# Gated linear attention with an ELU feed-forward on one core: late form for spans 4 and 5, another weight decode, another way to k over P, another order

## The chip, the cores and the metric

One core of one Trainium2 chip runs the whole program. The metric is device time in microseconds, the median of the runs shown. The kernel before takes 504.29 us (503.95 to 504.69, three runs).

## The reference

Attention with a decaying state, then a feed-forward block. For each of 4 x 8 heads, over 768 positions with head size 48:

```python
for t in range(S):
    state = alpha[:, :, t, :, None] * state + np.einsum('bhd,bhe->bhde', k[:, :, t], v[:, :, t])
    y[:, :, t] = np.einsum('bhd,bhde->bhe', q[:, :, t], state)
...
h = x @ w_in                                   # x: 3072 x 384, w_in: 384 x 2048
g = np.where(h > 0.0, h, np.exp(np.minimum(h, 0.0)) - 1.0)
return g @ w_out                               # w_out: 2048 x 384
```

`x` is the attention's output, the heads side by side. The arrays are float32, but the drawn weights are float64, and the kernel gets the float64 words.

## The kernel before, in words

**Attention by spans.** The 768 positions of a batch element are six spans of 128, so there are 24 spans, numbered 0 to 23. A span works on all eight heads at once, in four slices of two heads. Within it P is the running product of alpha (SC, L200, on DVE); k is divided by P and put in a form with the kernel's sign conventions (LN, EX on ACT; KA, KB on DVE or POOL; KC on DVE, L232), q is multiplied by P (SQ, L249 or L252). S multiplies k and q (PE, L330 or L314), MK masks the result (DVE, L347 or L342), U multiplies k, laid over rows, with v (PE, L376 or L358), UA, UB and UC move the state on (L393, L395, L424, L426), and Y gives the span's output (PE, L437 or L442), which XH and XL split in a high and a low float32r part (L496, L522) and XD (L529, a DMA) completes.

**Two forms.** `EARLY`, `QU` and `QS` are 6: spans 0 to 5 take the early form, in which a Y product is split in two, one for the state and one for the mask part (L437), and U and S run over one PSUM bank each. From span 6 on the late form runs Y as one product over 128 rows (L442), and U and S as four products at a time on the four quarters of the array (`U4`, `S4`, L358 and L314), but the masks, the state's steps and SQ come in halves of 48 or 64 rows, so that DVE issues them twice, and MK four times (L342).

**k over rows.** U wants k with positions on the rows. In spans 0 to 5 that is TP (PE, L266) and a copy (KN, ACT, L295). From span 6 on it is `blocks` (L276): DVE transposes 32-row blocks, 16 instructions a span, called as TA, TB or T.

**Feed-forward by blocks.** Two spans are one block of 256 positions, so there are 12 blocks b; the 2048 hidden units are eight parts j. A(b, j) is 18 products (L639), O(b, j) 12 (L690); between them RA and RB (ACT, L647, L652), RC (DVE, L657), GH (ACT, L663) and GL (DVE, L676) make the ELU and its high and low parts. Z writes a block's result.

**Weights.** F (L549) loads 768 KB of float64 words for each of 16 weight parts, two to a pair p of eight. DA, DB and DC (DVE, L565, L571, L577) put a float32 together from the two 32-bit halves of each word, for a whole pair at a time; WH (ACT, L603) and WL (POOL, some on DVE or ACT, L623, L621) split it in high and low parts. LC, CA and CB (L585, L590, L595) load all weights once more in 32 pieces and check their range on ACT; V and VP gather the checks.

**Order.** Nothing is scheduled on the chip or by a planner at build time. `START` and `STEADY` are tables of step names with arguments; the steps are called in that order, and each engine and each queue executes its instructions in the order in which they were called. `STEADY` describes one block's worth of work, with numbers relative to the block, and is repeated. All input DMAs are on SP's queue. X is a product of a constant into a spare bank that nobody reads (L126); it occupies PE before the first data have come. PSUM has eight buffers and the spans' q, k and alpha share three, so a step can also wait for a buffer.

Of the kernel before, what the change touches and what calls it, by code (L numbers as in the profile page):

```python
# [30 lines left out]
EARLY = 6  # L31
# [3 lines left out]
QU, QS = 6, 6  # L35

PAIRS = 10

# [14 lines left out]
WH.4 SC.4 WL.4 Y3.2 Y.2 UA.3 PC.3 RB.0.0 MK.3 XH.2 DA.3 SQ.4 DC.1 DB.3 YL.3 LN.4 XL.2 Y3.3 UB.3 A.0.2 LV.4
WH.3 EX.4 F.10 CA.0 F.8 WL.3 Y.3 A.0.3 XH.3 UC.3 DC.3 XL.3 L.5 F.12 RA.0.1 KA.4 KB.4 A.1.1 A.1.0 LV.5 F.11
RC.0.0 RB.0.1 RC.0.1 WH.7 GH.0.0 SC.5 DA.5 RA.0.2 GH.0.1 A.1.2 RB.0.2 DB.5 RA.1.0 KC.4 RC.0.2 WH.1 RB.1.0 F.14
GH.0.2 GL.0.0 RC.1.0 WL.1 RA.1.1 GL.0.2 A.1.3 RA.0.3 GL.0.1 RB.0.3 TP.4 UB.0 DA.4 PC.4 RB.1.1 WL.7 WH.5 KN.4
O.0.0 RC.0.3 O.0.1 GH.0.3 DB.4 U.4 WL.5 GL.0.3 RC.1.1 DC.4 RA.1.3 GH.1.1 S.4 LN.5 O.0.2 O.0.3 RB.1.3 DC.5 LV.6
L.6 WH.8 MK.4 UB.4 RA.1.2 EX.5 LV.7 GH.1.0 UA.4 RB.1.2 WL.8 GL.1.0 WH.9 KA.5 RC.1.2 CB.0 A.0.4 GH.1.2 GL.1.1
UC.4 WH.10 KB.5 RA.0.4 KC.5 O.1.0 RC.1.3 TP.5 GL.1.2 SQ.5 GH.1.3 LC.1 DA.6 CA.1 KN.5 WH.11 L.7 O.1.1 DB.6
RB.0.4 WL.10 U.5 PC.5 RC.0.4 GL.1.3 GH.0.4 UA.5 A.1.4 A.0.5 SC.6 RA.1.4 WL.11 LN.6 EX.6 KA.6 WL.9 DC.6 F.15  # L60
RB.1.4 RA.0.5 O.1.2 GL.0.4 WH.14 O.1.3 RC.1.4 RB.0.5 RC.0.5 GH.0.5 GH.1.4 S.5 KB.6 SC.7 KC.6 WH.12 Y.4 O.0.4
WL.12 GL.1.4 PC.6 LN.7 EX.7 WL.14 MK.5 GL.0.5 F.13 A.0.6 TB.6 A.0.7 CB.1 L.8 RA.0.6 A.1.5 DA.7 KA.7 TA.6 DB.7
# [18 lines left out]
MK.2.1 UC.2 XD.1 ZV.4 O.-4 XD.0 RC.-3 CB.-12 SC.4 RB.-2 A.-1 PC.3 GH.-3 RC.-2 A.0 LN.4 GL.-3 UA.3 EX.4 RA.-1
GH.-2 LC.-11 MK.3.0 L.6 MK.3.1 UB.3 CA.-11 A.1 RA.0 KA.4 L.5 RB.-1 GL.-2 RC.-1 A.2 RB.0 UC.3 CB.-11 RA.1 GH.-1
RC.0 O.-3 KB.4 RB.1 SC.5 KC.4 LC.-10 GL.-1 LN.5 GH.0 EX.5 RC.1 T.4.1 O.-2 A.3 VP.0 CA.-10 T.4.2 GL.0 GH.1 A.4
T.4.3 KA.5 O.0 RA.2 GL.1 RB.2 RA.3 CB.-10 LV.5 RC.2 PC.4 GH.2 KB.5 RB.3 GL.2 LC.-9 O.1 O.-1 KC.5 RA.4 O.2 SQ.4
T.5.2 CA.-9 RB.4 RC.3 CB.-9 RC.4 GH.3 T.5.1 GH.4 T.5.0 GL.3 T.4.0 T.5.3 LC.-8 SQ.5 Z.-1 GL.4
"""

@with_exitstack
def gla_elu_ffn(ctx: ExitStack, tc: tile.TileContext, qka, vv, vn, wgt, out):
    nc = tc.nc  # L90
# [861 lines left out]
```

## Time and profile before

| what | value |
|---|---|
| median of three runs | 504.29 us |
| the profiled execution itself | 503.54 us |
| its span, first to last instruction | 501.8 us |
| granted TensorE clock, mean | 1.000 |
| PE, DVE, ACT, POOL busy, share of the span | 98%, 77%, 58%, 26% |
| the chain of waits, share of PE | 95% |
| lines L639 and L690 in that chain | 40% and 40% |
| DMA, mean over the span | 122 GB/s |

The span is the time between the first and the last instruction; the execution's own time, 503.54, is 1.7 us longer. A busy PE is one that has a matmul in flight. The chain of waits goes back from the last instruction, at each step to what released it.

### The profile page before, as it was taken

What the parts mean: (1) busy time and instruction counts of PE and PEld (TensorE: products, weight loads), DVE (VectorE), ACT (ScalarE), POOL (GpSimd) and SP (SyncE); (2) the same over time, 40 slices, a digit from 0 to 9 for tenths busy, and PEclk for the clock granted to TensorE, in tenths of its full rate; (3) what the DMA queues carried; (4) which work ended last, traced back from release to release, by engine and by line L of the source; (5) the groups of instructions that cost most, each with busy time, mean ns of one, the idle gap of its engine ahead of it and who ended that gap; (6) DMA issues with size and microseconds to landing.
All of it is one profiled execution on the core that took longest, in us unless ns stands there. A gap on an engine that the chain in (4) does not pass through costs nothing.

```text
span 501.8 us, 13252 instructions
## 1 busy us (share of the span) xinstructions
PE 491.7 (98%) x5404; PEld 474.4 (95%) x5404; DVE 385.9 (77%) x807; ACT 289.7 (58%) x689; POOL 128.3 (26%) x109
## 2 busy tenths in 40 slices
PE   7999999999999999999999999999999999999996
PEld 3799999999999899999999999999999999999995
DVE  6989999989998579769969969769969878344321
ACT  3656786456460677746755756647755755454432
POOL 4125565443320302501501501501501500000000
PEclk9999999999999999999999999999999999999999
DMA  8999323213522145226245145235233321110001
GB/s 312 413 410 377 97 96 142 88 50 106 189 64 64 51 137 177 65 81 217 55 122 179 48 125 180 58 112 183 72 111 100 92 77 49 51 44 6 3 33 36
DMA packets 22403, 61.13 MB, mean 122 GB/s; under 512 B 2880, under 2 KB 9792, under 8 KB 22336
## 3 DMA queue, kind: packets, MB, share of 16 engines
q1 hardware_dynamic: 22048, 59.83, 36.3%
q8 instruction: 44, 0.72, 0.6%
q10 hardware_dynamic: 288, 0.39, 0.2%
q14 instruction: 23, 0.19, 0.1%
HBM read 53.53 MB, written 4.72 MB: 116 GB/s over the span
## 4 chain that ended last, share of the span: by engine, by line
PE 95%; DVE 2%; ACT 1%; issue 1%; ACTq 0%
PE h L639 40%; PE o L690 40%; PE y L442 4%; PE y L437 2%; PE q L314 2%; PE q L358 1%; PE u L376 1%; PE wp L126 1%; PE sc L330 1%; PE y L481 1%; PE tp L266 1%; DVE kn L276 0%; PE yl L437 0%; PE wd L612 0%; DVE st L342 0%
## 5 line engine op out<-in xcount | busy, mean ns | idle before, releaser
L639 PE MATMUL h<-xt,w 128*128 128x256 f32 x1728 | 215.3, 282 | 0.0
L639 PEld LDWEIGHTS h<-xt,w 128*128 128x128 f32 x1728 | 209.3, 188 | 2.3 <-issue 0.9
L690 PE MATMUL o<-w,gh 128*128 128x384 f32 x768 | 199.3, 341 | 0.8 <-ACT gh L663 0.8
L690 PEld LDWEIGHTS o<-w,gh 128*128 128x128 f32 x768 | 136.8, 188 | 1.7 <-ACT gh L663 1.0
L690 PE MATMUL o<-w,gl 128*128 128x384 f32 x384 | 130.0, 339 | 0.1
L663 ACT CAST gh<-h 128x512 fp32r<-128x512 f32 x96 | 56.0, 583 | 78.4 <-PE o L690 39.9
L676 DVE TENSOR_TENSOR gl<-h,gh 128x512 fp32r<-128x512 f32 x96 | 65.6, 687 | 35.6 <-ACT gh L663 34.4
L276 DVE STREAM_TRANSPOSE kn<-qka 32x128 f32<-32x128 f32 x288 | 87.1, 302 | 4.5
L647 ACT ACTIVATE r<-h 128x512 f32<-128x512 f32 x96 | 57.1, 596 | 47.7 <-PE h L639 39.7
L657 DVE SCALAR_TENSOR_TENSOR h<-r,h 128x512 f32<-128x512 f32 x96 | 64.6, 689 | 17.0 <-ACT r L652 16.2
L690 PEld LDWEIGHTS o<-w,gl 128*128 128x128 f32 x384 | 72.1, 188 | 0.4 <-DVE gl L676 0.4
L222 POOL TENSOR_TENSOR qka<-qka,R 128x512 f32<-128x512 f32 x19 | 26.2, 1378 | 163.9 <-DVE gl L676 116.4
L652 ACT ACTIVATE r<-r 128x512 f32<-128x512 f32 x96 | 59.4, 631 | 0.7
L252 POOL TENSOR_TENSOR st<-qka,P 64x512 f32<-64x512 f32 x36 | 42.8, 1190 | 21.7 <-DVE P L200 16.3
L342 DVE TENSOR_TENSOR st<-q,mask 64x256 f32<-64x256 f32 x72 | 30.4, 422 | 11.8 <-ACT vs L393 9.0
L200 DVE TENSOR_TENSOR_SCAN P<-qka,first 128x516 f32<-128x516 f32 x24 | 30.4, 1267 | 2.8 <-DMA qka<-in_qka_dram 2.3
L227 POOL TENSOR_TENSOR R<-P,R 128x512 f32<-128x512 f32 x20 | 24.2, 1211 | 27.2 <-DVE qka L222 25.8
L209 ACT ACTIVATE R<-P 128x512 f32<-128x512 f32 x24 | 15.2, 632 | 27.7 <-DVE P L200 27.7
L395 DVE TENSOR_TENSOR vs<-vs,q 48x192 f32<-48x192 f32 x30 | 10.5, 349 | 18.0 <-PE q L314 16.1
L495 ACT ACTIVATE y<-y 128x128 fp32r<-128x128 f32 x20 | 5.5, 276 | 29.7 <-PE y L442 26.4
L623 POOL TENSOR_TENSOR w<-spare,w 128x768 fp32r<-128x768 f32 x7 | 15.2, 2173 | 25.8 <-ACT w L603 25.8
L595 ACT ACTIVATE ck<-ck,lim 128x384 f32<-128x384 f32 x32 | 20.7, 646 | 0.1
(100 smaller groups left out, 421.6 us busy)
## 6 DMA issues: line engine op xcount, KB each, us to landing
qka<-in_qka_dram SPq DMA_DIRECT2D x22, 770.0 KB, 6.4
raw<-in_wgt_dram SPq DMA_DIRECT2D x16, 768.0 KB, 13.4
ck<-in_wgt_dram SPq DMA_DIRECT2D x32, 384.0 KB, 3.2
vs<-in_vv_dram SPq DMA_DIRECT2D x36, 192.0 KB, 4.3
out_dram<-ot SPq DMA_DIRECT2D x22, 192.0 KB, 1.9
vs<-in_vv_dram SPq DMA_DIRECT2D x6, 384.0 KB, 12.3
xt<-y SPq DMA_DIRECT2D x40, 48.0 KB, 2.3
qka<-in_qka_dram SPq DMA_DIRECT2D x2, 512.0 KB, 4.9
```

Of the source, the lines that this page charges most:

```text
L200: nc.vector.tensor_tensor_scan(out=P.rearrange("p n w -> p (n w)"), data0=t[:, 2 * NP * W:], data1=first.rearrange("p n w -> p (n w)"), in ...
L222: eng(KAV, i).tensor_tensor(out=d["kt"], in0=d["kt"], in1=d["R"], op=ALU.mult)
L252: eng(SQV, i).tensor_tensor(out=st[r, a], in0=d["q"][r], in1=pw(i)[r], op=ALU.mult)
L276: nc.vector.transpose(out=kn[32 * t:32 * t + 32, :, 32 * g:32 * g + 32], in_=d["kt"][32 * g:32 * g + 32, :, 32 * t:32 * t + 32])
L342: nc.vector.tensor_tensor(out=d["st"][r, a, :, c * C:(c + 1) * C], in0=d["s4"][a][o], in1=mask[o].unsqueeze(1).broadcast_to([64, NP, C]), ...
L639: nc.tensor.matmul(h[:, f, :], lhsT=t[:, wi, ws], rhs=x[:, c, xi, :], start=(f == 0 and k == 0), stop=(k == 8), skip_group_check=True)
L647: nc.scalar.activation(out=r, in_=d["h"], func=AF.Relu, scale=-1.0)
L652: nc.scalar.activation(out=d["r"], in_=d["r"], func=AF.Exp, scale=-1.0)
L657: nc.vector.scalar_tensor_tensor(out=d["h"], in0=d["r"], scalar=-1.0, in1=d["h"], op0=ALU.add, op1=ALU.max)
L663: nc.scalar.copy(out=gh, in_=d["h"])
L676: nc.vector.tensor_tensor(out=gl, in0=d["h"], in1=d["gh"].bitcast(F32), op=ALU.subtract)
L690: nc.tensor.matmul(o[:, 0:DM], lhsT=gt[:, f, ms], rhs=t[:, wi, f * DM:f * DM + DM], start=(j == 0 and f == 0 and k == 0), stop=(j == NJ - ...
```

## The change

Spans 4 and 5 go to the late form (`EARLY`, `QU`, `QS` are 4). Their U and S then share two PSUM banks, since `shared` gives separate ones only to spans 6 to 9. The decode works on bytes: the raw words are placed five bytes into their buffer, so that one aligned 32-bit word holds the bits from 24 to 55 of a float64 and the next one its top byte. DA shifts the first right by 5, DB makes sign and upper exponent from the top byte by a multiplication and an addition, DC shifts that left by 27 and joins the two. A third check of the weights' range joins the other two, so CB is two activations where it was one. From span 6 on k comes over rows by one DVE transposition of all 128 x 512 elements, T, and four DMAs of 64 KB on SP's queue, TM; U then reads it with a step of two elements. Both tables are new, and there are eight X products more ahead of the first TP.

```diff
-EARLY = 6
+EARLY = 4
 WARM = 12
-QU, QS = 6, 6
+QU, QS = 4, 4
 PAIRS = 10
+APART = (6, 7, 8, 9)
...
 START = """
-LA.0 LB.0 SC.0 LN.0 EX.0 LA.1 KA.0 KB.0 LB.1 SC.1 X.2 LV.0 LN.1 X.2 KC.0 F.2 SQ.0 EX.1 F.0 TP.0 KN.0 S.0 U.0
...
+X.2 LA.0 LB.0 LA.1 X.2 X.1 LV.0 SC.0 LN.0 EX.0 KA.0 SC.1 LN.1 X.1 EX.1 KB.0 KC.0 X.1 LB.1 X.1 X.1 X.1 X.1 X.1 PC.0 TP.0
...
+    @tok
+    def T(i):
+        d = win[i]
+        tk = d["tk"] = d["R"].rearrange("p n w -> p (n w)").rearrange("p (t b x c) -> p t b x c", t=4, b=2, c=2)
+        nc.vector.transpose(out=tk.rearrange("p t b x c -> p (t b) c x"),
+                            in_=d["kt"].rearrange("p n (j t) -> p t n j", t=4))
+
+    @tok
+    def TM(i):
+        d = win[i]
+        kn = d["kx"] = work.tile([128, 2, 2, 64, 2], F32, name="kn", tag="kn")
+        for g in range(4):
+            nc.sync.dma_start(out=kn[:, :, g // 2, g % 2 * 32:g % 2 * 32 + 32].rearrange("p b x c -> p b (x c)"),
+                              in_=d["tk"][32 * g:32 * g + 32].rearrange("p t b x c -> p (t b) (x c)"))
...
-        if i < PAIRS or "q4" not in d:
+        if i in APART or "q4" not in d:
...
-                nc.tensor.matmul(d["u"][x][64 * a:64 * a + D, n, :], lhsT=d["kn"][r, n, a, 0:D],
+                nc.tensor.matmul(d["u"][x][64 * a:64 * a + D, n, :], lhsT=d["kx"][r, n // 2, a, 0:D, n % 2] if "kx" in d else d["kn"][r, n, a, 0:D],
...
-            raw[p] = wtile(p, [128, 2, WCH, 2], I32, "raw")
-        nc.sync.dma_start(out=raw[p][:, k].rearrange("p k two -> p (k two)"), in_=wgt[f].bitcast(I32))
+            raw[p] = wtile(p, [128, 2, 8 * WCH + 64], U8, "raw")
+        nc.sync.dma_start(out=raw[p][:, k, 5:5 + 8 * WCH], in_=wgt[f].bitcast(U8))
...
+    def parts(p):
+        t = raw[p][:, :, 8:8 + 8 * WCH]
+        words = t.bitcast(I32).rearrange("p k (c two) -> p k c two", two=2)
+        return words[:, :, :, 0], words[:, :, :, 1], t.rearrange("p k (c x) -> p k c x", x=8)[:, :, :, 4]
...
-        nc.vector.tensor_scalar(out=mi, in0=hi32, scalar1=3, scalar2=0x3FFFFFFF,
-                                op0=ALU.logical_shift_left, op1=ALU.bitwise_and)
+        nc.vector.tensor_single_scalar(out=wm[p].bitcast(I32), in_=parts(p)[0], scalar=5,
+                                       op=ALU.logical_shift_right)
...
-        nc.vector.scalar_tensor_tensor(out=mi, in0=lo32, scalar=29, in1=mi,
-                                       op0=ALU.logical_shift_right, op1=ALU.bitwise_or)
+        word, top = parts(p)[1:]
+        nc.vector.tensor_scalar(out=word, in0=top, scalar1=1.125, scalar2=-63.4375, op0=ALU.mult, op1=ALU.add)
...
-        nc.vector.scalar_tensor_tensor(out=mi, in0=hi32, scalar=-2 ** 30, in1=mi,
-                                       op0=ALU.bitwise_and, op1=ALU.bitwise_or)
+        nc.vector.scalar_tensor_tensor(out=mi, in0=parts(p)[1], scalar=27, in1=mi,
+                                       op0=ALU.logical_shift_left, op1=ALU.bitwise_or)
...
-        nc.scalar.activation(out=t, in_=t, func=AF.Relu, scale=-1.0, bias=lim, accum_out=chk_w[:, 1, f:f + 1])
+        for k, (sign, bias) in enumerate(((1.0, lim[:, 1:2]), (-1.0, lim[:, 0:1]))):
+            nc.scalar.activation(out=t[:, :, k], in_=t[:, :, 1], func=AF.Relu, scale=sign, bias=bias,
+                                 accum_out=chk_w[:, k, f:f + 1])
```

The order on the engines differs as follows at three places. The first is PE ahead of the first feed-forward product (`h`, L639 before, L638 after): `u` is U, `sc` is S of an early span, `tp` is TP; the last digits of `qka` name one of the three input buffers, 119, 120, 121 before and 120, 121, 122 after. Before:

```order
L500 MATMUL wd<-w_305,minus 128x384
L500 MATMUL y<-xt,minus 128x384
L376 MATMUL u<-vs_107,kn 64x48 x16
L330 MATMUL sc<-st,qka_121 64x64 x16
L639 MATMUL h<-xt,w_305 128x256 x36
L266 MATMUL tp<-ident,qka_119 128x128 x4
L330 MATMUL sc<-st,qka_119 64x64 x16
```

and after:

```order
L496 MATMUL wd<-w_311,minus 128x384
L496 MATMUL y<-xt,minus 128x384
L372 MATMUL u<-vs_107,kn 64x48 x16
L326 MATMUL sc<-st,qka_120 64x64 x16
L269 MATMUL tp<-ident,qka_120 128x128 x4
L326 MATMUL sc<-st,qka_122 64x64 x16
L638 MATMUL h<-xt,w_311 128x256 x18
```

S and TP of span 3 stand ahead of the first A now, and S of span 2 behind them.

The second place is PE at U, S and Y of spans 4 and 5, among the first O products (`o`); `q` is the late form of U (48x48) and S (64x64). Before, span 4's U and S, and span 5's S with span 4's Y:

```order
L690 MATMUL o<-w_622,gl 128x384
L376 MATMUL u<-vs_105,kn 64x48 x16
L330 MATMUL sc<-st,qka_120 64x64 x16
L690 MATMUL o<-w_734,gh 128x384 x2
...
L330 MATMUL sc<-st,qka_121 64x64 x16
L437 MATMUL y<-st,vs_105 64x64 x32
L690 MATMUL o<-w_939,gh 128x384 x2
```

and after, span 4's S and U ahead of the first O, and span 5's:

```order
L638 MATMUL h<-xt,w_421 128x256 x54
L269 MATMUL tp<-ident,qka_121 128x128 x4
L638 MATMUL h<-xt,w_421 128x256 x18
L310 MATMUL q<-st,qka_121 64x64 x16
L354 MATMUL q<-vs_105,kn 48x48 x16
L689 MATMUL o<-w_647,gh 128x384 x2
...
L354 MATMUL q<-vs_106,kn 48x48 x8
L310 MATMUL q<-st,qka_122 64x64 x16
L689 MATMUL o<-w_943,gh 128x384 x2
```

The products are the late ones, and seven A stand ahead of the first O.

The third place is the way of k for span 6, on DVE and on SP's queue (`kn` is k over rows, `R` the buffer through which it goes). Before, on DVE:

```order
L276 STREAM_TRANSPOSE kn<-qka_119 32x4x32 x8
L565 TENSOR_SCALAR wm<-raw_1088 128x1536
L276 STREAM_TRANSPOSE kn<-qka_119 32x4x32 x8
L571 SCALAR_TENSOR_TENSOR wm<-raw_1088,wm 128x1536
L657 SCALAR_TENSOR_TENSOR h<-r,h 128x512
```

and after, DVE's piece and SP's:

```order
L675 TENSOR_TENSOR gl<-h,gh 128x512
L276 STREAM_TRANSPOSE R<-qka_120 128x8x2x32
L675 TENSOR_TENSOR gl<-h,gh 128x512
...
L174 DMA qka_122<-in_qka_dram 128x1540
L284 DMA kn<-R 128x2x64 x4
L525 DMA xt<-y_1307 16x6x128 x2
```

Sixteen DVE instructions became one, and four DMAs stand on SP's queue between the load of a later span and XD.

## Rows read from the trace of the kernel before

**Rows 1.** The page, part 1: busy time of the engines.
```profile
PE 491.7 (98%) x5404; PEld 474.4 (95%) x5404; DVE 385.9 (77%) x807; ACT 289.7 (58%) x689; POOL 128.3 (26%) x109
```

**Rows 2.** Busy time by stretch: length, PE, PEld, DVE, ACT, POOL, clock, DMA share, GB/s.
```profile
10.00:25.00 15.00, 13.97 (x284) 11.40 (x283) 13.79 (x18) 9.05 (x24) 2.74 (x2) 1.00 1.02 414
25.00:80.00 55.00, 55.00 (x663) 52.43 (x663) 52.88 (x62) 38.06 (x82) 27.03 (x14) 1.00 0.62 224
...
200.00:490.00 290.00, 290.00 (x3031) 285.54 (x3030) 208.08 (x481) 168.49 (x418) 56.27 (x48) 1.00 0.29 90
```

**Rows 3.** The waits of PE: waiter, releaser, us in total, times, longest.
```profile
PE wp L126 <- DVE first L120: 2.1, 1, 2.1
PE tp L266 <- issue: 1.4, 1, 1.4
PE o L690 <- ACT gh L663: 0.8, 1, 0.8
```

**Rows 4.** The chain of waits in time: start us, us, what.
```profile
9.66 0.63 PE tp L266 x4
...
60.15 1.14 PE u L376 x29
...
61.35 0.94 PE sc L330 x31
...
73.52 0.60 PE u L376 x16
...
82.77 1.08 PE sc L330 x32
83.85 1.92 PE y L437 x64
...
98.64 2.06 PE y L437 x64
...
103.04 2.12 PE o L690 x12
...
110.10 0.51 PE q L358 x32
110.60 0.49 PE q L314 x32
...
120.58 2.02 PE y L442 x64
```

**Rows 5.** The timeline of the first ten us: start us, us, engine, line, what.
```profile
6.75 0.15 PEld L126 LDWEIGHTS <-first 128*128 128x128 bf16 x1 [0.27 <-issue]
...
7.18 0.54 PEld L126 LDWEIGHTS <-first 128*128 128x128 bf16 x3 [0.28 <-issue]
...
8.89 0.66 DVE L232 SCALAR_TENSOR_TENSOR qka<-R,qka 128x512 f32<-128x512 f32 x1
```

**Rows 6.** Groups by line and shape: xcount | busy us, mean ns | idle before, releasers.
```profile
L276 DVE STREAM_TRANSPOSE kn<-qka 32x128 f32<-32x128 f32 x288 | 87.1, 302 | 4.5
...
L342 DVE TENSOR_TENSOR st<-q,mask 64x256 f32<-64x256 f32 x72 | 30.4, 422 | 11.8 <-ACT vs L393 9.0 <-PE q L314 1.3
...
L395 DVE TENSOR_TENSOR vs<-vs,q 48x192 f32<-48x192 f32 x30 | 10.5, 349 | 18.0 <-PE q L314 16.1 <-PE q L358 1.6
...
L571 DVE SCALAR_TENSOR_TENSOR spare<-raw,spare 128x1536 int32<-128x1536 int32 x4 | 7.0, 1755 | 0.1
...
L565 DVE TENSOR_SCALAR spare<-raw 128x1536 int32<-128x1536 int32 x4 | 4.3, 1076 | 0.3 <-DMA raw<-in_wgt_dram 0.3
L347 DVE TENSOR_TENSOR st<-sc,mask 128x512 f32<-128x512 f32 x6 | 4.1, 683 | 0.4 <-PE sc L330 0.4
```

**Rows 7.** The page, part 5, the check's activation; part 6, XD's DMAs: KB each, us to landing.
```profile
L595 ACT ACTIVATE ck<-ck,lim 128x384 f32<-128x384 f32 x32 | 20.7, 646 | 0.1
...
xt<-y SPq DMA_DIRECT2D x40, 48.0 KB, 2.3
```

**Rows 8.** The timeline at the second pair's decode.
```profile
23.05 0.96 DVE L565 TENSOR_SCALAR spare<-raw 128x1536 int32<-128x1536 int32 x1 [0.28 <-DMA raw<-in_wgt_dram]
```

More of the change, by code (lines that the diff above doesn't have):

```diff
@@ L11 @@
 I32 = mybir.dt.int32
+U8 = mybir.dt.uint8
 AF = mybir.ActivationFunctionType
@@ L53 @@
[L53 to L62, printed above, removed]
@@ L81 @@
[L81 to L85, printed above, removed]
+CA.-12 A.-3 Y.0 CB.-12 Y.1 XH.1 U.2 XL.1 S.2 XH.0 RA.-3 UA.2 RB.-3 A.-1 MK.2.0 UB.2 RC.-3 A.-2 GH.-3 LC.-11 UC.2 XL.0
@@ new lines @@
+CA.-11 O.-5 SC.4 XD.1 XD.0 MK.2.1 V.0 CB.-11 RA.-2 RB.-2 O.-4 S.3 LC.-10 U.3 LN.4 GL.-3 A.2 RA.-1 RB.-1 O.-3 UA.3 A.0
+RC.-2 RA.2 MK.3.1 CA.-10 RB.2 L.5 UB.3 RC.-1 UC.3 GH.-1 MK.3.0 L.6 EX.4 SC.5 SQ.4 GH.-2 RA.0 LN.5 RC.2 KA.4 A.1 GL.-1
+RB.0 RC.0 KB.4 GH.0 A.3 CB.-10 RA.1 RA.3 GL.-2 O.-2 GL.0 LV.4 O.0 RB.3 LC.-9 EX.5 KA.5 GH.2 RB.1 KC.4 PC.4 LV.5 RC.1
+T.4 ZV.4 RC.3 O.-1 TM.4 A.4 GH.1 GH.3 GL.1 CA.-9 CB.-9 RA.4 LC.-8 O.1 Z.-1 KB.5 GL.2 RB.4 SQ.5 RC.4 KC.5 PC.5 O.2 GH.4
+VP.0 T.5 GL.3 TM.5 GL.4
@@ L146, in gla_elu_ffn @@
     nc.vector.memset(chk_y[:, 1, 0:DIRECT], 0.0)
-    lim = const.tile([128, 1], F32, name="lim")
-    nc.vector.memset(lim, 2.0 ** -14)
+    lim = const.tile([128, 2], F32, name="lim")
+    nc.vector.memset(lim[:, 0:1], 2.0 ** -14)
+    nc.vector.memset(lim[:, 1:2], 2.0 ** -23 - 2.0)
     win = [{} for _ in range(NWIN)]
@@ L266, in TP @@
             nc.tensor.transpose(out=tp[:, n, :], in_=d["kt"][:, n, :], identity=ident)
-    def blocks(i, gs):
+    @tok
+    def T(i):
         d = win[i]
-        if "kn" not in d:
-            d["kn"] = work.tile([128, NP, 2, 64], F32, name="kn", tag="kn")
-        kn = d["kn"].rearrange("p n a x -> p n (a x)")
-        for g in gs:
-            for t in range(4):
-                nc.vector.transpose(out=kn[32 * t:32 * t + 32, :, 32 * g:32 * g + 32],
-                                    in_=d["kt"][32 * g:32 * g + 32, :, 32 * t:32 * t + 32])
-    @tok
-    def T(i, g):
-        blocks(i, (g,))
-    @tok
-    def TA(i):
-        blocks(i, (0, 1))
-    @tok
-    def TB(i):
-        blocks(i, (2, 3))
+        tk = d["tk"] = d["R"].rearrange("p n w -> p (n w)").rearrange("p (t b x c) -> p t b x c", t=4, b=2, c=2)
+        nc.vector.transpose(out=tk.rearrange("p t b x c -> p (t b) c x"),
+                            in_=d["kt"].rearrange("p n (j t) -> p t n j", t=4))
+    @tok
+    def TM(i):
[4 more added lines that the diff above has]
+                              in_=d["tk"][32 * g:32 * g + 32].rearrange("p t b x c -> p (t b) (x c)"))
     @tok
@@ L547, in F @@
         if p not in raw:
-            raw[p] = wtile(p, [128, 2, WCH, 2], I32, "raw")
-        nc.sync.dma_start(out=raw[p][:, k].rearrange("p k two -> p (k two)"), in_=wgt[f].bitcast(I32))
-    def words(p):
-        return raw[p][:, :, :, 0], raw[p][:, :, :, 1], wm[p].bitcast(I32)
+            raw[p] = wtile(p, [128, 2, 8 * WCH + 64], U8, "raw")
[4 more added lines that the diff above has]
+        return words[:, :, :, 0], words[:, :, :, 1], t.rearrange("p k (c x) -> p k c x", x=8)[:, :, :, 4]
     @tok
@@ L589, in CA @@
         t = ck[f].bitcast(F32)[:, :, 1]
-        nc.scalar.activation(out=t, in_=t, func=AF.Abs, accum_out=chk_w[:, 0, f:f + 1])
+        nc.scalar.activation(out=t, in_=t, func=AF.Abs, accum_out=chk_w[:, 2, f:f + 1])
     @tok
     def CB(f):
-        t = ck.pop(f).bitcast(F32)[:, :, 1]
-        nc.scalar.activation(out=t, in_=t, func=AF.Relu, scale=-1.0, bias=lim, accum_out=chk_w[:, 1, f:f + 1])
+        t = ck.pop(f).bitcast(F32)
+        for k, (sign, bias) in enumerate(((1.0, lim[:, 1:2]), (-1.0, lim[:, 0:1]))):
+            nc.scalar.activation(out=t[:, :, k], in_=t[:, :, 1], func=AF.Relu, scale=sign, bias=bias,
+                                 accum_out=chk_w[:, k, f:f + 1])
     @tok
```

56 lines of the change are left out of this document (31 added, 25 removed).

## The prediction

> **What bounds the kernel.** I read the page first: PE is busy for 491.7 of 501.8 us, DVE for 386, ACT for 290 [rows 1]. A busy PE need not be a bound one, so the stretches come next: from 25 to 80 us and from 200 to 490 PE has no idle time at all, while DVE goes from 52.9 busy us of 55 in the first to 208 of 290 in the second [rows 2]. Then the waits: PE waits for its first constant (2.1 us), once before the first transposition (1.4) and once in mid-program for a high part that ACT makes (0.8); three more waits come to about one us [rows 3]. The chain in time says the same: between 30 us and the last output it is almost wholly PE's own products [rows 4]. So time is won only where PE gets less to execute or where one of these few waits goes. DVE work that goes wins nothing by itself: its cover is PE's own work. It can only make a wait less likely, and DVE is close to full between 25 and 80.
>
> The sum is made against the profiled execution of 503.54 us; the median is 504.29, 0.75 above it. I take the difference from the one and put it on the other.
>
> **Spans 4 and 5 on PE.** Before: U of span 4 costs 1.14, its S 0.94, U of span 5 0.60, its S 1.08, the two Y 1.92 and 2.06 [rows 4]; together 7.74 us. In the late form U is 0.51 and S 0.49, and two Y in a row 2.02, so 1.01 each [rows 4]. Span 5 is the last of its batch element and has half the U products, between 0.25 and 0.51; I take 0.3, nearer the half. That gives 0.51 + 0.49 + 0.3 + 0.49 + 2.02 = 3.81, so 3.9 us go. All of it is on the path, since PE has no idle time there. PE changes from small products to large ones 31 times in both orders, so nothing is added there.
>
> The late form gives this back on DVE. Four masks at 0.42 replace one at 0.68, +1.0 a span; UA, UB and UC are issued twice, +0.35 each [rows 6]; span 5's SQ is two instructions instead of one, +0.7 by the row of the mask on as many elements, and UC of span 3 already writes span 4's halves, +0.35. That is some 4.5 us between 25 and 100, and it is hidden as long as DVE keeps ahead.
>
> **Decode.** DA has one operation instead of two on the same words, and I leave it at 1.0 to 1.08. DC stays a two-input instruction. DB was one, at 1.76 [rows 6], and is now a one-input one with byte input; no row shows that. Bounds are DA's 1.0 and the old 1.76. I take 1.1, since DA is the one-input instruction with the same strides. Five pairs are decoded in the tight stretch, so DVE gets back between nothing and 3.8 us there. Off the path, unless DVE falls behind (first rival).
>
> **k over rows.** From span 6 on 16 instructions of 0.30, 4.8 us a span, 87.1 in all [rows 6], become one. No row has a 128 x 512 transposition; 128 elements take 0.30 and a 128 x 512 mask 0.68, so 0.6 is the floor, four old ones in a row (1.2) the ceiling, and I take 1.2 for its wide steps. DVE loses some 65 us after 85 us. On the path this is worth what PE waits there: 0.8, the one wait in mid-program, for GH [rows 3]. GH follows RC on DVE, and I put its lateness down to DVE's string of transpositions; so I count all of it: -0.8. TM issues four DMAs a span on SP's queue, behind T, and the later loads, XD and Z stand behind them. The nearest row is XD, two DMAs of 48 KB at 2.3 us to landing [rows 7]; for four of 64 KB I estimate less than twice that, 4 us from T to U. Two product groups hold it: T of the later span stands ahead of a GL for which an O waits, and behind the start of that O PE has two O (2.12 each) and an S (0.49) before U, 4.7 us. DVE, idle for 82 us of 290 there even before [rows 2], should have T done well before this.
>
> **ACT.** The third check adds 32 activations of 0.65 us [rows 7] and as many reads of an accumulator, about 27 us over a program in which ACT is idle for 210. Between RA and GH such an activation delays an O by at most its own length; the O's own distance to its A hides it. Nothing.
>
> **The start.** Eight more warming products go behind the 16. They were issued every 0.43 us and at the end three within 0.54, the last ending at 8.21 [rows 5]; the granted clock stands at 1.00 in that stretch, yet the pace of 512 columns in 0.43 is that of the level of 1.2 GHz and the later one that of 2.4. So eight more cost 1.7 at the late pace, 3.4 at the early one, and PE is free at 9.9 to 11.6. KC of span 0 ends at 9.55 [rows 5] and TP begins at 9.66 [rows 4]: +0.3 to +2.0. I take +0.3, since the added products follow the fast ones. Against it, PE idles 1.03 us between 10 and 25 [rows 2], and the new order puts span 1's TP and S and span 3's S and TP where PE waited: between nothing and -1.03, and I take -0.7, as most of these waits were short ones behind a single span's steps. Net -0.4.
>
> **Sum.** -3.9 - 0.8 - 0.4 = -5.1: 498.4 for the profiled execution, 499.2 for the median.
>
> **Rivals.** First: **DVE takes part back.** In 25 to 80 DVE idles 2.1 us [rows 2]; the late form adds up to 4.5 there and a slow DB returns nothing, so PE could wait up to 2.4 us, mostly for GL ahead of the first O, which now stand behind seven A. The new order issues the decode of pair 1 in pieces between other steps, which speaks against it. Time: 504.3 - 5.1 + 2.4 = 501.6. Chance 0.20.
>
> Second: **U reads k more slowly.** It now loads weights with a step of two elements, which no row shows. U is 0.51 a span on PE in 18 late spans, so between nothing and a doubling, +8.4; half of that, +4.2, gives 503.4, no change. What speaks against it: weights are loaded beside other products, and PEld is not full. The Trainium skill ("SBUF — State Buffer", section "Door 1: The DMA port swizzle") has lines of 16 bytes, with full rate for two or more hits in one; two float32 of step two lie in a line, so by it U costs nothing more. Chance 0.06.
>
> Third, on the other side: **the raw loads get slower.** They now land at an odd byte. From 10 to 25 us the DMA engines are full at 414 GB/s [rows 2], and the second pair's decode waited 0.28 us for its load [rows 8], so loads come just in time. In the new queue 384 KB less stand ahead of that pair, 0.95 us, which leaves 0.7 us of slack on four loads of 768 KB, 7.6 us at 414 GB/s. It decides from about 9% on: at double the time the third pair, after six loads (11.4 us), comes 10.7 us late, and with some 3 us of other work to put in its place the result is about 507. No row has an odd byte. The Trainium skill ("DMA: Bandwidth & Descriptors", section "How a descriptor splits into AXI transactions") lets a transaction start only at a multiple of 256 bytes, so a row of 6144 takes 25 instead of 24; an estimate from it is 4%, below the point. Chance 0.08.
>
> Fourth: **k comes late to U.** If TM takes 6 us and T is only just in time, each block loses about 1.3 us, with nine blocks +11.7; at half of that the time is 505. The Trainium skill (the same page, section "Specifications") has a read-modify-write below 512 bytes, and TM moves runs of 256; by it TM is slower than XD's row, with no figure for how much. DVE's idle share of a quarter after 200 us speaks against T being late. Chance 0.06.
>
> That the change doesn't do what it says is no rival: fewer and shorter products are in the order.
>
> **Numbers.** Forecast 0.60, rivals 0.20, 0.06, 0.08, 0.06. A measurement of this kernel tells about 0.2% from no change, 1.0 us. Faster: the forecast, the first rival, some of the second and fourth, 0.82. Same: 0.06. Slower: the third and most of the fourth, 0.12. The forecast's own range is 497.0 to 501.2. Its upper end has the warming products at +2.0 and no idle time of the start won back but 0.4. Its lower end counts from the profiled execution, 498.4, and takes off all idle time of the start and the three small waits, 1.4. For 8 in 10 it must take in the first rival and most of the second: 497.0 to 503.8.
>
> **What would show it.** Right: U, S and Y of spans 4 and 5 at about 0.5, 0.5 and 1.0 in the chain; no wait of PE for GH after 30 us; the first TP at about 10; T at 0.6 to 1.2 and DVE's busy time below 330; landing of TM under 5 us. Wrong: PE waits between 30 and 65 us (first rival); U's groups longer than 0.6 (second); DVE idle before L562 released by a raw load, with several us (third); PE idle in every block before U, released by `kn` (fourth).

## The result and the profile after

The changed kernel takes **496.41 us** (median of four runs, 496.07 to 498.33), the kernel before 504.12 beside it (503.95 to 504.69): a ratio of 0.9855, with an interval of 0.9834 to 0.9876. That is 7.7 us faster. The direction was forecast, the size was not: 499.2 us had been the forecast and 497.0 the lower end of the range. Two single runs of the experiments below, 508.17 us with spans 4 and 5 undone and 503.39 us with 16 warming products, had a mean granted clock of 0.984 and 0.985 and are left out of the medians and ratios given there.

The profiled execution is the longest of the four, 498.33 us with a span of 496.7. The busy times of the changed kernel, from the page, answer to [rows 1]:

```profile
PE 487.2 (98%) x5348; PEld 470.7 (95%) x5348; DVE 320.9 (65%) x550; ACT 315.6 (64%) x753; POOL 130.9 (26%) x110
```

Two of the stretches of [rows 2], in the same columns (length, PE, PEld, DVE, ACT, POOL, clock, DMA share, GB/s):

```profile
25.00:80.00 55.00, 55.00 (x698) 52.35 (x697) 50.58 (x69) 37.89 (x80) 27.92 (x17) 1.00 0.70 239
200.00:490.00 290.00, 289.98 (x3034) 285.97 (x3032) 166.96 (x304) 187.93 (x461) 55.76 (x46) 1.00 0.34 99
```

The waits of PE, all that the view lists, answer to [rows 3]:

```profile
PE wp L128 <- DVE first L122: 2.1, 1, 2.1
PE tp L269 <- issue: 0.7, 1, 0.7
PE tp L269 <- DVE qka L235: 0.3, 1, 0.3
```

After the first transpositions PE waits for nothing that the view lists; the 0.8 us for GH is gone. DVE has lost 65 us and is still the fuller of the helpers between 25 and 80 us, with 50.6 of 55.

The chain in time (start, us, what) answers to [rows 4]: the first TP, S and U of span 4, U and S of span 5, their two Y, and three O in a row late in the program.

```profile
10.30 0.63 PE tp L269 x4
...
51.59 0.62 PE q L310 x32
52.22 0.36 PE q L354 x32
...
78.42 0.49 PE q L354 x16
78.91 0.49 PE q L310 x31
...
90.20 1.08 PE y L438 x32
...
97.75 1.08 PE y L438 x32
...
424.62 6.33 PE o L689 x36
```

The six groups of spans 4 and 5 come to 4.12 us where they were 7.74 [rows 4], so 3.6 went there. The last row is the one to stop at. Three O in a row are 6.33 here, and three times the O of [rows 4] would be 6.36. The feed-forward products are the same instructions as before, 96 A and 96 O, and the change does not touch them. Yet they run a little faster, in the whole program.

The DVE groups by line and shape answer to [rows 6], and two DMA groups of the page (KB each, us to landing) to [rows 7]:

```profile
L276 DVE STREAM_TRANSPOSE R<-qka 128x512 f32<-128x512 f32 x18 | 20.0, 1110 | 5.7 <-ACT R L239 5.7
...
L569 DVE TENSOR_SCALAR raw<-raw 128x1536 int32<-128x1536 uint8 x8 | 7.9, 991 | 0.0
```

```profile
raw<-in_wgt_dram SPq DMA_DIRECT2D x16, 768.0 KB, 11.0
...
kn<-R SPq DMA_DIRECT2D x72, 64.0 KB, 2.2
```

T takes 1.11 us (estimate 1.2), DB 0.99 (1.1), and each DMA of TM lands 2.2 us after its issue.

**Where the time went.** The end of the chain, before and after:

```profile
490.74 6.37 PE o L690 x36
497.11 0.02 issue
```

```profile
479.80 10.54 PE o L689 x60
490.34 0.02 issue
```

PE's last product ends at 497.11 us before and at 490.34 after, 6.8 us earlier. Spans 4 and 5 account for 3.6, the wait for GH for 0.8 and the start for about 0.3: the first A begins at 30.67 us against 29.44, but behind span 3's S and TP, which stood behind it before with 1.08 and 0.44 us (that chain, at 34 us). That is 4.7. Some 2 us are left, in no place of their own. They are spread over the A and O of the whole program.

**Behind PE's last product.** From there to the end of the profiled execution 6.4 us pass before (503.54 less 497.11) and 8.0 after (498.33 less 490.34). This remainder holds the last copy, the output's last DMA and the end of the program, and over the traces of this case it takes 6.0 to 7.2 us in the kernels with the old order and 5.8 to 8.0 in those with the new one. So two medians can differ by a microsecond or two without any difference in PE's work, and where a small difference matters below, the end of PE's last product stands beside the time.

### The profile page after: what moved, and what is told of

The parts are those of the page before. It is cut to its first block, busy times and chain, and to the rows that moved or that the text cites. A ratio compares the mean times of both kernels' runs of the same rounds, so it can differ in the third digit from the quotient of the medians.

```text
span 496.7 us, 13064 instructions
## 1 busy us (share of the span) xinstructions
PE 487.2 (98%) x5348; PEld 470.7 (95%) x5348; DVE 320.9 (65%) x550; ACT 315.6 (64%) x753; POOL 130.9 (26%) x110
## 4 chain that ended last, share of the span: by engine, by line
PE 98%; DVE 0%; issue 0%; ACT 0%; DVEq 0%
PE h L638 42%; PE o L689 41%; PE y L438 4%; PE q L310 2%; PE q L354 2%; PE wp L128 2%; PE y L433 1%; PE sc L326 1%; PE u L372 1%; PE tp L269 1%; PE y L477 1%; PE wd L611 1%; PE yl L433 0%; PE u L398 0%; PE wd L496 0%
## 5 line engine op out<-in xcount | busy, mean ns | idle before, releaser
L638 PE MATMUL h<-xt,w 128*128 128x256 f32 x1728 | 215.5, 281 | 0.0
L638 PEld LDWEIGHTS h<-xt,w 128*128 128x128 f32 x1728 | 209.3, 188 | 1.6
L255 POOL TENSOR_TENSOR st<-qka,P 64x512 f32<-64x512 f32 x38 | 47.3, 1244 | 102.5 <-issue 95.0
L593 ACT ACTIVATE ck<-ck,lim 128x384 f32<-128x384 f32 x64 | 41.7, 651 | 1.7
L338 DVE TENSOR_TENSOR st<-q,mask 64x256 f32<-64x256 f32 x80 | 33.7, 422 | 8.5 <-PE q L310 4.6
L230 POOL TENSOR_TENSOR R<-P,R 128x512 f32<-128x512 f32 x20 | 28.1, 1407 | 39.7 <-DVE qka L225 38.4
L203 DVE TENSOR_TENSOR_SCAN P<-qka,first 128x516 f32<-128x516 f32 x24 | 35.1, 1463 | 1.8 <-DMA qka<-in_qka_dram 1.4
L276 DVE STREAM_TRANSPOSE R<-qka 128x512 f32<-128x512 f32 x18 | 20.0, 1110 | 5.7 <-ACT R L239 5.7
L514 DVE TENSOR_TENSOR y<-y,y 128x128 fp32r<-128x128 f32 x20 | 5.8, 288 | 25.9 <-ACT xt L492 25.6
L212 ACT ACTIVATE R<-P 128x512 f32<-128x512 f32 x24 | 15.0, 625 | 11.5 <-DVE P L203 11.5
L239 ACT ACTIVATE R<-P 128x512 f32<-128x512 f32 x24 | 15.1, 630 | 10.7 <-DVE qka L235 10.7
L438 PE MATMUL y<-st,vs 128*64 128x64 f32 x640 | 21.3, 224 | 0.0
## 6 DMA issues: line engine op xcount, KB each, us to landing
vs<-in_vv_dram SPq DMA_DIRECT2D x4, 384.0 KB, 10.1
```

Source lines behind the costliest of these rows:

```text
L203: nc.vector.tensor_tensor_scan(out=P.rearrange("p n w -> p (n w)"), data0=t[:, 2 * NP * W:], data1=first.rearrange("p n w -> p (n w)"), in ...
L255: eng(SQV, i).tensor_tensor(out=st[r, a], in0=d["q"][r], in1=pw(i)[r], op=ALU.mult)
L338: nc.vector.tensor_tensor(out=d["st"][r, a, :, c * C:(c + 1) * C], in0=d["s4"][a][o], in1=mask[o].unsqueeze(1).broadcast_to([64, NP, C]), ...
L438: nc.tensor.matmul(out[64 * a:64 * a + m], lhsT=lhs(i, c, a)[:, n * D:n * D + m], rhs=d["st"][:, a, n, c * C:(c + 1) * C], start=start, st ...
L593: nc.scalar.activation(out=t[:, :, k], in_=t[:, :, 1], func=AF.Relu, scale=sign, bias=bias, accum_out=chk_w[:, k, f:f + 1])
L638: nc.tensor.matmul(h[:, f, :], lhsT=t[:, wi, ws], rhs=x[:, c, xi, :], start=(f == 0 and k == 0), stop=(k == 8), skip_group_check=True)
```

## The experiments

Theories on the part that is left: **places** (the raw tile has grown from 12288 to 12416 bytes per partition, and every buffer behind the first weight tile lies elsewhere in SBUF), **DVE** (PE streams faster because DVE does less beside it), **order** (what stands next to what on PE). The experiments also undo or do alone the parts of the sum. Each time is set against the kernel before on the same chip.

### The places alone

```diff
-            raw[p] = wtile(p, [128, 2, WCH, 2], I32, "raw")
...
+            raw[p] = wtile(p, [128, 2, WCH + 8, 2], I32, "raw")
...
```

The load and the decode use the first `WCH` words as before.

> The kernel before, with 64 unused bytes behind each half of a raw weight tile, as the changed kernel has them; the instructions, their order and sizes stay as they were, only the places of the weight, x, gh and gl tiles in SBUF shift by 128 bytes a tile. Theory 'places': the feed-forward products of the changed kernel run a little faster (12 O products 2.09 us against 2.12, 1728 and 1152 of them over the program) because the tiles lie elsewhere; then this kernel is 2.0 to 2.6 us faster than before, and an O in the chain takes 2.09. Theory 'DVE' (PE streams faster because DVE works less beside it) and theory 'order' (it comes from what stands next to what on PE): no change, within 0.5 us, an O at 2.12.

Measured: 502.04 us against 504.37, ratio 0.9949 (0.9921 to 0.9978). Unused bytes make the kernel 2.3 us faster. The chain of the kernel before, late in the program, and the same piece of the padded one:

```profile
435.27 8.48 PE o L690 x48
```

```profile
433.09 8.41 PE o L690 x48
```

Four O take 8.41 instead of 8.48, and PE's last product ends at 494.55 us, 2.6 earlier. The instructions and their order are those of the kernel before, so the places alone give as much as is left to explain, with nothing changed for DVE or in the order.

### Distance or spacing

One unused tile ahead of the spans' buffers moves xt, gh and gl, and leaves the weight tiles where they are. `n` is 32 (128 bytes), 64 (256 bytes) or 16 (64 bytes).

```diff
+    gap = work.tile([128, n], F32, name="gap", tag="gap", bufs=1)
+    nc.gpsimd.memset(gap, 0.0)
```

> The kernel before, with one unused tile of 128 bytes per partition ahead of the spans' buffers, so that xt, gh and gl lie 128 bytes further on and the weight tiles stay where they were. From the by-part pace of the padded kernel: an O whose weights lie (modulo 256) 96 bytes behind gh takes 1.945 us from its first to its last product, one at 224 takes 1.907 to 1.930, and an A 2.00 to 2.02 against 1.98. Theory 'distance' (the place of the weights against gh and xt modulo 256 decides): every part is at 224 here, all O at 1.91 to 1.93, and the gain is about double that of the padded kernel, 4 to 6 us. Theory 'spacing' (it was the 12288 bytes between the weight tiles): no change, within 0.5 us.

> The same with 256 bytes. Theory 'distance modulo 256': every part is at 96 as in the kernel before, and nothing changes, within 0.5 us, O at 1.945. A theory in which any shift of these buffers helps: 2 us or more faster.

> The kernel before, with an unused tile of 64 bytes ahead of the spans' buffers: the weight tiles at distance 32 from gh and xt modulo 256 (96 and 224 were seen). If the distance matters in steps of 128 only, 504 or 499.5 like one of them; if in finer steps, a third time, and the pace of O between or beyond 1.91 and 1.945.

Measured: 128 bytes 499.48 against 504.20, ratio 0.9899 (0.9882 to 0.9917); 256 bytes 504.05, ratio 1.0003 (0.998 to 1.0027); 64 bytes 502.29 against 504.27, ratio 0.9965 (0.9952 to 0.9977). Two A and four O in the chain of the kernel before, with 128 bytes and with 64:

```profile
431.04 4.23 PE h L639 x36
435.27 8.48 PE o L690 x48
```

```profile
427.57 4.20 PE h L641 x36
431.77 8.33 PE o L692 x48
```

```profile
429.74 4.26 PE h L641 x36
434.00 8.33 PE o L692 x48
```

The spacing of the weight tiles is not it. By part, worked out from the starts of the products in the traces (first to last of the 12 products of an O, median over the blocks between 175 and 480 us; the distance is weights minus gh, in bytes modulo 256, from the addresses that the program gives its tiles; part 4 is left out where other work stands inside it):

| kernel | parts at 96 | us | parts at 224 | us |
|---|---|---|---|---|
| before | all | 1.942 to 1.946 | none | |
| 256 bytes | all | 1.943 to 1.946 | none | |
| padded | 2, 3, 6, 7 | 1.939 to 1.945 | 0, 1, 5 | 1.907 to 1.930 |
| the changed kernel | 2, 3, 6, 7 | 1.939 to 1.945 | 0, 1, 4, 5 | 1.909 to 1.921 |
| 128 bytes | none | | all | 1.907 to 1.909 |

In one and the same kernel the parts at 224 are fast and those at 96 are not. The weights' own addresses don't decide it, for with 128 bytes they are those of the kernel before; nor do gh's, which modulo 256 are the same in the kernel before and the padded one. With 64 bytes all are at 32: O is then as fast as at 224, 1.908 to 1.913 us, and A is not faster than before. So the time between that of 96 and that of 224 is not a pace in between: one kind of product gains and the other does not.

### Which tiles

The same 128 bytes ahead of r, gh and gl only, and ahead of gl only:

```diff
+    gap = gpool.tile([128, 32], F32, name="gap", tag="gap", bufs=1)
+    nc.gpsimd.memset(gap, 0.0)
```

> The kernel before, with the unused 128 bytes ahead of r, gh and gl only: xt, and so both operands of an A, stay where they were, while O's gh and gl go to distance 224 from the weights. Theory 'operands' (the distance of a product's own two operands decides): O at 1.91, A at 2.00 to 2.02 as before, and 2.0 to 3.0 us faster than before. Theory 'writers' (what decides is where ACT and DVE write r, gh and gl beside a running product): A gains too, and the time is that of the shift of all buffers, 4 to 5 us faster.

> The same ahead of gl only, which is an operand of 4 of an O's 12 products. Theory 'operands': those products and the ones that run beside their loads gain, O at 1.92 to 1.935, A as before, 0.7 to 1.8 us faster than before. Theory 'writers': little or nothing, or A gains as well.

Measured: the first 501.19 against 504.25, ratio 0.9929 (0.9913 to 0.9945), O at 1.906 to 1.925. Two A in the chain take 4.23 us as before (medians of parts 0 to 5: 1.995 to 2.001, before 2.005 to 2.021, with the 128 bytes ahead of all 1.984 to 1.987; where the weights of an A are not at 224, single ones take about 2.00 or 2.01 to 2.02 in both kernels, and which of the two no run explains). The second 503.66, ratio 0.9982 (0.997 to 0.9994), O at 1.926 to 1.929, in part 3 at 1.945. The first gains a little more than was expected, 3.1 us, the second a little less, 0.6, or 0.9 by the ratio. So it is the distance between the two operands of a product, and not where other engines write: moving O's operands helps O, and moving gl, one of two stationary operands of O, brings part of it.

### The changed kernel with all places slow, and all fast

```diff
-            raw[p] = wtile(p, [128, 2, 8 * WCH + 64], U8, "raw")
+            raw[p] = wtile(p, [128, 2, 8 * WCH + 128], U8, "raw")
```

puts every part at 96 again. The gap of 128 bytes on top of it puts every part at 224.

> The changed kernel with 128 unused bytes behind each half of a raw tile instead of 64, so that every weight tile is at distance 96 modulo 256 again, as in the kernel before; all else is the changed kernel's. Theory 'distance': the pace of the old kernel, O at 1.945, and the gain over before falls from 7.7 to 5.0 to 5.6, which is what the sum had without the places, 5.1. Otherwise: 7.2 to 8.0.

> The same with one unused tile of 128 bytes ahead of the spans' buffers, so that every weight tile is at 224. Theory 'distance': all O at 1.91 to 1.92, all A at 1.98, and 2.0 to 3.0 us faster than the changed kernel: a gain of 9.7 to 10.7 over before, which makes it the fastest of them. Otherwise 7.2 to 8.0.

Measured: all slow 500.17 against 504.20, ratio 0.9912 (0.9893 to 0.9931), 4.0 us faster than before, 4.4 by the ratio, with O at 1.938 to 1.945; all fast **494.69**, ratio 0.9814 (0.9793 to 0.9835), 9.5 us faster than before and the fastest of all kernels here. Its chain:

```profile
423.05 6.25 PE o L691 x36
```

Both gains are below what was expected, by 1.0 and 0.2 us. With all places slow DVE has as little to do as in the changed kernel, and PE's order is the changed one, yet O has the old pace: the theories on DVE and order fall here. PE's last product ends at 492.66 us with all slow, 4.5 earlier than before and 2.3 later than in the changed kernel. So the change without the luck of its places is worth 4.0 to 4.5 us, against 5.1 in the sum, and the places that it has by chance are worth 2.3.

### Spans 4 and 5

Undone in the changed kernel:

```diff
-EARLY = 4
+EARLY = 6
-QU, QS = 4, 4
+QU, QS = 6, 6
```

> The changed kernel with spans 4 and 5 in the early form again (EARLY, QU, QS at 6), at its own order and places. By the sum 3.9 us more on PE, by the pieces of the two chains 3.6: a gain over before of 3.8 to 4.1 instead of 7.7, with U, S and Y of spans 4 and 5 at 7.7 us together and the rest as in the changed kernel. If the late form had brought its gain by something else than PE's own work (fewer PSUM banks held, more room on DVE), the loss would be over 4.5 or under 2.5.

Measured: 501.21 against 504.27, ratio 0.9936 (0.9917 to 0.9956); the changed kernel has 0.9855, so 4.1 us are lost by ratio. PE's last product ends at 493.64 us, 3.3 later than in the changed kernel; as the first A begins at 30.08, 0.6 earlier, PE needs 3.9 more between the two. The chain:

```profile
51.00 1.08 PE sc L326 x32
52.08 1.20 PE u L372 x32
...
79.15 0.53 PE u L372 x13
...
79.75 0.94 PE sc L326 x31
...
91.49 2.06 PE y L433 x64
...
100.02 2.06 PE y L433 x64
```

With two bits of span 5's U and S that are left out (0.07) these are 7.94 us, against 4.12: 3.8 for this part.

Done alone in the kernel before, with the old tables:

```diff
-EARLY = 6
+EARLY = 4
-QU, QS = 6, 6
+QU, QS = 4, 4
-        if i < PAIRS or "q4" not in d:
+        if 6 <= i < PAIRS or "q4" not in d:
```

> The kernel before, with EARLY, QU and QS at 4 and a shared pair of banks for spans 4 and 5, its order tables as they are. The sum of the prediction has 3.9 us less on PE for this part, and the pieces of the changed kernel's chain make it 3.6: 3.6 to 3.9 us faster than before, with U, S and Y of the two spans at 0.4, 0.5 to 0.6 and 1.0 to 1.1. First rival (DVE's added masks and state steps hold PE up): 1.2 to 2.5 faster only, with waits of PE between 45 and 110 us. All theories on the rest of the gain: the pace of O stays at 2.12.

Measured: 514.40 against 504.37, ratio 1.0189 (1.0143 to 1.0236): 10 us *slower*, outside every expectation. In the late form the load of v is two DMAs instead of one, and the second is issued 3 us after the first: SP's queue waits there until an earlier raw load has landed (2.9 us in the list of its waits). The issues on SP's queue (start, us, line, what), of the kernel before and of this one:

```profile
33.52 0.33 SPq L187 DMA_DIRECT2D vs<-in_vv_dram  x1
35.37 2.22 SPq L549 DMA_DIRECT2D raw<-in_wgt_dram  x2
```

```profile
34.64 0.47 SPq L189 DMA_DIRECT2D vs<-in_vv_dram  x1
38.07 0.47 SPq L190 DMA_DIRECT2D vs<-in_vv_dram  x1
39.01 1.14 SPq L549 DMA_DIRECT2D raw<-in_wgt_dram  x2
```

The two raw loads go out 3.6 us later, and the chain shows what follows: 12.92 us of load, then DVE for most of the way until an A of PE at 85 us. The decode is in this stretch, and so are the late form's four masks of span 4 and its doubled steps of the state.

```profile
39.01 12.92 DMA raw<-in_wgt_dram
...
52.05 0.97 DVE spare L565
...
68.20 0.42 DVE st L342
...
85.30 3.79 PE h L639 x18
```

PE is busy 49.96 of the 55 us between 25 and 80, and the granted clock there is 0.97 instead of 1.00. The A at 85.30, behind a wait of 2.53 us, takes 3.79, where 2.12 is usual; the granted clock between 86 and 89 us is 0.50, the level of 1.2 GHz. The two loads are F.11 and F.14. In the changed START they stand ahead of span 5's load of v, in the old one behind it. How much of the 10 us is the loads' and how much DVE's added work, the first rival's mechanism, is not shown: no run moves the loads alone.

### k over rows

Done alone in the kernel before, T and TM where the first of a span's transpositions stood:

```diff
-WL.12 GL.1.4 PC.6 LN.7 EX.7 WL.14 MK.5 GL.0.5 F.13 A.0.6 TB.6 A.0.7 CB.1 L.8 RA.0.6 A.1.5 DA.7 KA.7 TA.6 DB.7
+WL.12 GL.1.4 PC.6 LN.7 EX.7 WL.14 MK.5 GL.0.5 F.13 A.0.6 T.6 TM.6 A.0.7 CB.1 L.8 RA.0.6 A.1.5 DA.7 KA.7 DB.7
...
```

> The kernel before with k laid over rows by T and TM, each where the first of the span's transpositions stood; all else, the places of the tiles too, as before. By the sum the wait of 0.8 for GH goes and nothing else: 0.5 to 1.0 us faster, DVE busy about 320 us instead of 386. A rival: the wait for GH has another cause, and nothing changes. Another: TM's DMAs come late behind other DMAs of the queue, and PE waits for kn ahead of U: slower.

Measured: 511.87 against 504.27, ratio 1.0156 (1.0121 to 1.0191): 7.6 us *slower*, the direction of the third expectation but not its cause, for no wait for `kn` is in the list. The wait for GH of 0.8 is gone from it, and this is in the chain:

```profile
138.20 1.03 DVE R L273
139.28 0.68 SPq L281
...
142.82 2.35 DMA xt<-y
...
145.95 3.90 PE h L632 x18
```

T is late, the four DMAs of TM stand on SP's queue until it is done, XD stands behind them, and an A waits 2.40 us for XD. At 155 us the same happens to a load of v, and U waits for v, 1.9 us in two pieces. Behind both waits the clock is lower; the stretch of the first A (columns of [rows 2]):

```profile
145.00:150.00 5.00, 4.05 (x20) 4.08 (x21) 1.42 (x1) 0.39 (x3) 2.39 (x2) 0.66 0.96 303
```

Between 146.1 and 149.4 us the granted clock is 0.50, and again between 163.1 and 166.5. The A behind the first wait takes 3.90 us and the one behind the second 3.42, where 2.12 is usual. The waits and what these two A take longer come to 7.4 us; less the wait for GH that is 6.6 of the 7.6.

Undone in the changed kernel, 16 transpositions at the place of T and no DMAs:

```diff
...
-        nc.vector.transpose(out=tk.rearrange("p t b x c -> p (t b) c x"),
-                            in_=d["kt"].rearrange("p n (j t) -> p t n j", t=4))
...
+        for g in range(4):
+            for t in range(4):
+                nc.vector.transpose(out=kn[32 * t:32 * t + 32, :, 32 * g:32 * g + 32],
+                                    in_=d["kt"][32 * g:32 * g + 32, :, 32 * t:32 * t + 32])
...
```

> The changed kernel with k laid over rows by 16 DVE transpositions a span again, at the place of T, and no DMAs for it; DVE gets some 67 us more work. Theory 'DVE': the products run at the old pace again, an O at 2.12, and the gain over before falls from 7.7 to about 5.3, or to 4.5 with a wait for GH as at 168 us before. Theories 'places' and 'order': an O stays at 2.09, gain 6.9 to 7.7; if the one wait for GH came from the string of transpositions, as the sum has it, it is back with 0.8.

Measured: 540.55 against 504.37, ratio 1.0696 (1.0649 to 1.0744), 44 us slower than the changed kernel; no theory had that. PE's waits:

```profile
PE o L688 <- DVE gl L674: 16.6, 8, 2.6
PE q L353 <- issue: 10.7, 7, 2.5
```

In the changed STEADY the two T stand as single steps close to the block's end. A string of 16 instructions, 4.8 us, in the same place holds up GL eight times and U seven times. Two O in an undisturbed piece take 4.20 us, and the parts of O have the changed kernel's pace (1.91 to 1.92 us in the undisturbed parts at 224, 1.94 in those at 96), so DVE's load does not slow the products: what it costs are these waits, and the clock behind them (0.97 in 200 to 490). The theory on DVE falls here too.

### The decode

The old DA, DB and DC in the changed kernel, with aligned loads and raw tiles of 12288 bytes, so with all places slow:

```diff
-            raw[p] = wtile(p, [128, 2, 8 * WCH + 64], U8, "raw")
-        nc.sync.dma_start(out=raw[p][:, k, 5:5 + 8 * WCH], in_=wgt[f].bitcast(U8))
+            raw[p] = wtile(p, [128, 2, WCH, 2], I32, "raw")
+        nc.sync.dma_start(out=raw[p][:, k].rearrange("p k two -> p (k two)"), in_=wgt[f].bitcast(I32))
...
```

> The changed kernel with the old decode (DA, DB, DC on 32-bit halves, loads at an aligned byte, raw tiles without the 64 bytes, so that the weight tiles lie 12288 bytes apart again). By the sum the decode is worth nothing by itself, and the first rival's condition comes 0.8 us a pair nearer: gain 7.7 to 6.5. Theory 'places': the pace of O goes back to about 2.12 and the gain falls to 5.1 to 5.7. Theories 'DVE' and 'order': O stays at 2.09.

Measured: 503.27 against 504.37, ratio 0.9959 (0.9933 to 0.9985), a smaller gain than any of the expectations. Set beside the changed kernel with slow places (500.17) the new decode is worth 3.1 us, 2.4 by the ratios and 2.7 by the end of PE's last product (495.32 against 492.66), where the sum had nothing. The chain shows DVE on the path ahead of the first A:

```profile
25.66 1.67 DVE spare L567
...
27.85 1.75 DVE spare L573
...
30.35 1.15 PE sc L326 x32
31.50 2.31 PE h L637 x18
```

The first A begins at 31.50 instead of 30.24 in the kernel with slow places, and a GH is waited for, 0.7 us at 61 us, another one than before's at 168. In the changed order DVE's room of this stretch has been spent.

### The warming products

```diff
-X.2 LA.0 LB.0 LA.1 X.2 X.1 LV.0 SC.0 LN.0 EX.0 KA.0 SC.1 LN.1 X.1 EX.1 KB.0 KC.0 X.1 LB.1 X.1 X.1 X.1 X.1 X.1 PC.0 TP.0
+X.2 LA.0 LB.0 LA.1 X.2 LV.0 SC.0 LN.0 EX.0 KA.0 SC.1 LN.1 EX.1 KB.0 KC.0 LB.1 PC.0 TP.0
```

> The changed kernel with 16 warming products as before, not 24. By the sum the eight cost 0.3 us at the first TP and nothing else hangs on them: this kernel is 0 to 0.5 us faster than the changed one. A rival: without them PE's products after the first TP run at the slow pace for some time, and this kernel is 0.5 to 3 us slower; seen in the duration of the first TP, S and U groups.

Measured: 497.22 against 504.27, ratio 0.985 (0.9831 to 0.987), not to be told from the changed kernel's 0.9855. The first TP starts at 9.53 us, 0.77 earlier than in the trace of the changed kernel, the first A 0.76 earlier, and PE's last product ends 0.7 earlier; groups are no longer than with 24. But of the traces here six have the same 24 products ahead of the same first TP, and it starts at 9.69, 9.73, 9.80, 9.87, 10.30 and 10.69 us. So the eight products cost between 0.2 and 1.2, with a median of 0.3.

```profile
9.53 0.63 PE tp L269 x4
...
29.91 2.33 PE h L638 x18
```

## Why the prediction was right in direction and short in size

- **Spans 4 and 5, -3.9:** right. With this part undone the chain's six groups have 3.8 more, PE from the first A to the last product 3.9, and the time 4.1.
- **The wait for GH, -0.8:** right in what it is worth; the wait is gone, in the changed kernel and with T and TM alone. That fits the string of transpositions as its cause, but neither run changes the string alone.
- **The start, -0.4:** about right as a net, -0.3 in the profiled execution. The first TP stands 0.64 later there than before, where I took 0.3; over six traces the median is 0.2, with 0.0 to 1.0. This term is no better known than that.
- **The sum, -5.1:** it stands to be compared with the changed kernel at the old distances, -4.0 to -4.5. It was 0.6 to 1.1 too large there, about what a measurement can tell.
- **The step that failed** is the sentence that time is won only where PE gets less to execute or where one of its few waits goes. It puts the duration of a large product at what it was, without a reason. I priced the new raw tile, under **Decode** and in the third rival, by its instructions and its odd first byte, and not by its size. It is 128 bytes larger per partition, moves half of the parts to another distance between weights and gh or xt, and their A and O run faster: 2.3 us with the padding alone, 2.3 between the changed kernel with slow places and as it is by the end of PE's last product (2.9 by the ratios, 0.0057 x 504). The sum had no term for it, the range's lower end of 497.0 has none either, and without it the time would lie within the range. That half of the parts became fast is luck: no part of the change was meant to do it.
- **What no term could have had:** of the 7.7 us PE's last product has 6.8; the rest lies behind it, where executions differ by up to two. That the profiled execution, 498.33, meets the 498.4 of the sum is such a coincidence: PE was 1.7 us ahead of the sum and the remainder 1.6 longer than before.
- **"DVE work that goes wins nothing by itself":** true only of the old order, in which it is spent on nothing. In the new one the decode is worth 2.4 to 3.1 us and the single T 44, since the order has been written for a DVE that has this room. The parts are not a sum: two of them, done alone in the old order, cost 10.0 and 7.6 us.
- **The first rival** (DVE takes part back) did not come: PE has no listed wait after 30 us, and DVE idles 4.4 us in 25 to 80. With the old decode it does come, and in the late form done alone it has a part.
- **The second** (strided reads of k) did not come: between 200 and 300 us the chain has U at 0.36 to 0.52 us, before at 0.36 to 0.51. That PEld is not full was a weak ground against it: PEld is busy 285.54 of 290 us [rows 2].
- **The third** (loads at an odd byte) did not come: raw loads land 11.0 us after their issue, 9.7 to 10.4 in the other kernels with the odd byte, 10.1 in the same order with aligned loads and the old decode (13.4 in the kernel before, with another queue), and the wait of [rows 8] has no counterpart. The extra transaction of the Trainium skill ("DMA: Bandwidth & Descriptors", section "How a descriptor splits into AXI transactions") costs nothing that these rows show.
- **The fourth** (k late to U) is not in the changed kernel, and not with T and TM alone either, where no wait for `kn` is listed. What costs the time there is what the prediction names and puts at nothing: XD and the loads stand behind TM on SP's queue. T was late, and A waited for XD and U for v.

## What to carry to other kernels

Before a change is summed up, compare where the tiles lie: in this program a tile that grows by 128 bytes moves all that are allocated behind it, and where PE is bound, the distance between the two operands of its products can be worth as much as the edit itself (here 4.7 us of 504 for one unused tile). Try that tile first; it costs one run. And price a step's DMAs by what stands behind them on their queue: an edit that is good in a new order can be bad in the old one, so a part that is undone or done alone tells of the part and its order together. And for differences of a microsecond, compare where PE's last product ends: the rest of an execution varied by two here.

## What the hardware showed that was not expected

- **The distance between a product's two operands.** An O product, 128 x 128 with 384 columns, takes 176.8 ns from start to start where the weights lie 96 bytes (modulo 256) behind gh (1.945 us over 11 steps), and 173.4 at 224 (1.907 us): 1.9%. For the 18 products of an A it is 2.00 to 2.02 us against 1.98 to 1.99 (weights minus xt). 256 bytes more change nothing. At 32 an O is as fast as at 224, and an A is as slow as at 96. With only gl moved, O's products differ by their place in the pattern: 171, 176 and 180 ns. The Trainium skill ("TensorE: Matmul & The Clock Gate", section "Step-by-step: what each phase is for") has two independent read ports, so that loading the next weights takes nothing from the running product. By that one would not expect the places of the two operands to matter; the runs differ by up to 5 us, and the measurement decides. What happens inside no run here shows, and only the distances 32, 96 and 224 were tried.
- **The clock behind a wait.** An A that follows a wait of 2.40 us took 3.90 us instead of 2.12, with a granted clock of 0.50, the level of 1.2 GHz, between 146.1 and 149.4 us. Of the 7.6 us that T and TM cost alone, the slower products behind the two waits are some 3.1, and the list of waits does not show them.
